# List products in the bank of the transposed values, the first softmax begun in step 23 and its sums spread over the last routing

## Chip, cores and metric

One core of a Trainium2 chip runs the whole kernel. The metric is device time in microseconds for one launch; the kernel before took 370.91 us in the median of three runs (368.12 to 375.25).

## What is computed

Three stages on 3,072 tokens (batch 4 x 768) of width 384 (8 heads x 48):

```python
# 1. linear attention with a decaying state, per (batch, head)
y[:, :, t] = r_t @ (state + u*k_t v_t^T);   state = w*state + k_t v_t^T
# 2. MoE, one of 8 experts per token, only where x @ w_skip > 0
probs  = softmax(xc @ w_gate);  e = argmax;   x = xc + probs[e] * relu(xc @ w1[e]) @ w2[e]
# 3. soft MoE with 32 slots: d is a softmax over the tokens (axis 0)
logits = x @ phi;  d = softmax(logits, axis=0);  slots = d.T @ x
out    = softmax(logits, axis=1) @ experts(slots)
```

## The kernel before

The order of the instructions on every engine is written out by hand (a manual schedule): each engine runs its instructions in the order in which the program emits them, and semaphores hold it where data or a buffer is not ready.

**The first loop** (`for i in range(NT)`, 24 steps) does the attention. Step i takes 128 positions of one batch row. On TensorE it emits `scores(i)` (L630, tile sc; then L635), `trx(i-2)` (L722, turns finished values; ScalarE copies them to x), `bonus(i)` (L652), `inter(i-1)` (L703), `upd(i)` (L649) and `av(i-1)` (L713). VectorE does `prep` (L612, L613), `past` (L676) and `amask` (L683), GpSimd the products of L615, L621, L659 and L671 and the one-hot masks `hots` (L756). Between them the routing of stage 2 goes on for groups of four steps: `route1` (L789, tile lgt), `route2` (tile lgp), `route2b`, `route3`, `places`/`gates` and `route4` (L908 to L910, emitted in steps 9, 13, 17 and 21). `gathered(g)` (L762) multiplies the tokens' numbers with their one-hot masks, for four groups of steps; the products land in PSUM as tile lip, and ScalarE casts them (L764). It is emitted right behind `bonus` in steps 13, 17 and 22 and once more behind `av` in step 22.

**PSUM banks** are shared by name. Tag "r" is one bank: lgt, lgp, lip, c4pt and others take it in turn, and a new tile waits until the last reader of the tile before it is done. In groups 0 to 3 the tile lgp also holds small scratch values (`spare`), and `route4` reads one of them (m) in L909. Tag "t" is another single bank: `trx` takes it in every step, and its only reader is ScalarE's copy (L723).

**The softmax over tokens** is built in pieces. For the first 16 steps' tokens the greatest logits are turned (L1030, c4pt, in bank "r"), reduced (L1004), spread over a diagonal (L1006, dgt), and after the loop multiplied by ones (L1105, mrt) so that every partition has them; then GpSimd subtracts (L1117), ScalarE takes Exp (L1121), and a `Weighted` object (L122, tile dpst) sums x with these weights in 16 products. The last eight steps' tokens form a second group, `gv` (c4pv, mrpv, tile dpsv).

**Last routing and start of the experts.** After the loop the last two rows are routed: `direct` (L809), `route2b(6)`, `route3(6)`, masks `hots(6)` on VectorE, `listed` (L773), the list idg (L1125); GpSimd gathers the rows of expert 0 by it (L1148, tile xg), `gtr(0)` (L1201) turns them, and `mm1` (L1213 to L1216) begins the 32 blocks of the expert phase, with `act` (hh on ScalarE, hlo on VectorE, L1224) and `mm2` (L1238 to L1240). `lows` (L956) makes the low halves of four weight blocks (early[0] to early[3]: a and b of block 0, a and b of block 1) ahead of the phase. `warm` (L492) issues products whose results nobody reads.

Of the kernel before, what the change touches and what calls it, by code (L numbers as in the profile page):

```python
# [8 lines left out]
F32 = mybir.dt.float32  # L9
# [3 lines left out]
AF = mybir.ActivationFunctionType  # L13
ALU = mybir.AluOpType
AX = mybir.AxisListType
# [4 lines left out]
P = 128  # L20
# [5 lines left out]
CAP = 256  # L26
# [439 lines left out]
def tile_main(ctx, tc, rk, kv, wu, wcat, phi, w1, w2, v1, v2, r_in, k_in, v_in, w_in, u_in, wcn, out, dbg=None, force=False):  # L466
    nc = tc.nc
# [3 lines left out]
    mk = fst.enter_context(tc.tile_pool(name="mk", bufs=1, side="right"))  # L471
# [16 lines left out]
    def warm(pool, tag, n):  # L488

        wp = pool.tile([P, 2, 4 * P], F32, tag=tag, name="wp")[:, 0] if tag == "y" else pool.tile([P, 4 * P], F32, tag=tag, name="wp")  # L490
        for _ in range(n):
            nc.tensor.matmul(wp, ones, ones.rearrange("p (o n) -> p o n", o=1).to_broadcast([P, 4, P]), start=True, stop=True)  # L492
# [168 lines left out]
    def moved(j):  # L661
        t = T[j]
        if j < NT - B:
            t["us"] = sp[j][1] if j < B else wk.tile([PR, 4, D], F32, tag="us", name=f"us{j}")
            nc.scalar.copy(t["us"], t["up"])
# [12 lines left out]
    def amask(j):  # L678
        t = T[j]
        if "at" not in t:  # L680
            past(j)
        at = t["at"]
        nc.vector.copy_predicated(  # L683
            at,
            ident_i.rearrange("s (a o t) -> s a o t", a=1, o=1).to_broadcast([P, 2, 4, P]),
            t["dtk"].rearrange("s (p o r) -> s r p o", o=1, r=32)[:, 0:2].to_broadcast([P, 2, 4, P]),
        )
# [17 lines left out]
    def av(j):  # L705
        t = T[j]
        c, b = divmod(j, B)
        yv, kvt, at = t["yv"], t["kv"], t["at"]
        for p in range(4):
            for f in range(2):  # L710
                h, g = 2 * p + f, f ^ (p < 2)
                m = 64 if c == 0 and f == 0 else D
                nc.tensor.matmul(yv[64 * f : 64 * f + m, p // 2, p % 2, :], kvt[:, 1, h * D : h * D + m], at[:, g, p, :], start=(c == 0 and p % 2 == 0), stop=(p % 2 == 1))  # L713
        if b == 0:
            yts[c] = ry.tile([PR, 4, B, P], F32, tag="yt", bufs=2, name=f"yt{c}")
        nc.scalar.copy(yts[c][:, :, b, :].rearrange("d (k q) t -> d k q t", k=2), yv)  # L716
# [21 lines left out]
    def tokens(g, eng):  # L738

        j0, nb = GR[g]  # L740
        o = tok[g % 2] if g < 4 else tok8[:, j0 - 16 : j0 - 16 + nb]
        sh = [P, nb, 2, E]
        eng.tensor_mul(
            o[:, :, 0:16].rearrange("t b (r e) -> t b r e", r=2),
            RT[g]["oh"].rearrange("t b (o e) -> t b o e", o=1).to_broadcast(sh),
            tj[:, :, j0 : j0 + nb].rearrange("t r (b o) -> t b r o", o=1).to_broadcast(sh),
        )
# [9 lines left out]

    def gathered(g):

        li = ps.tile([P, CAP], F32, tag="r", name=f"lip{g}")  # L760
        for b in range(B):
            nc.tensor.matmul(li[32 * b : 32 * b + 32, :], tok[g % 2][:, b, :], HOT[g][:, b, :], start=True, stop=True)  # L762
        LI.append(ry.tile([P, CAP], BF16, tag="li", name=f"li{g}"))
        nc.scalar.copy(LI[g], li)  # L764
# [63 lines left out]
    def route2b(g):  # L828
        c, (j0, nb) = g, GR[g]
        sh = [P, nb, E]  # L830
        r = RT[c]
        lg = r["lg"]
        if g < 6:
            nc.vector.tensor_add(lg, lg, r["lgp"][:, :, 64:106])
        else:
            lg = r["lgp"]
        gl = lg[:, :, 0:E]
        mx = spare(c, "mx", 42, 43)
        nc.vector.tensor_reduce(mx, gl, axis=AX.X, op=ALU.max)
        m = r["m"] = spare(c, "m", 43, 44) if j0 < 16 else m8[:, j0 - 16 : j0 - 16 + nb]  # L840
        nc.vector.tensor_scalar(m, lg[:, :, 8:9], 0.0, None, op0=ALU.is_gt)
        dd = rt.tile(sh, F32, tag="dd", name=f"dd{c}")
        nc.vector.tensor_sub(dd, gl, mx.to_broadcast(sh))
        wm = spare(c, "wm", 44, 52)
        nc.vector.tensor_mul(wm, w8.rearrange("t (o e) -> t o e", o=1).to_broadcast(sh), m.to_broadcast(sh))
        ex = r["ex"] = rt.tile(sh, F32, tag="ex", name=f"ex{c}")
        nc.scalar.activation(ex, dd, AF.Exp)
        t8 = spare(c, "t8", 52, 60)
        nc.vector.scalar_tensor_tensor(t8, dd, 0.0, wm, op0=ALU.is_equal, op1=ALU.mult)
        m2 = rt.tile([P, nb, 1], F32, tag="m2", name=f"m2{c}")  # L850
        nc.vector.tensor_reduce(m2, t8, axis=AX.X, op=ALU.max)
        oh = r["oh"] = rtile(g, "oh", oh8, BF16)
        nc.vector.scalar_tensor_tensor(oh, t8, 0.5, m2.to_broadcast(sh), op0=ALU.max, op1=ALU.is_equal)
# [20 lines left out]
    def gates(g):  # L874
        j0, nb = GR[g]
        se = spare(g, "se", 61, 62)
        nc.vector.tensor_reduce(se, RT[g]["ex"], axis=AX.X, op=ALU.add)
        yield
        nc.vector.tensor_scalar(se, se, 1.0e-9, None, op0=ALU.add)
        yield  # L880
        nc.vector.reciprocal(gt[:, j0 : j0 + nb], se)
        yield

    def places(g):
        j0, nb = GR[g]
        r = RT[g]
        r2 = rt.tile([P, nb, E], F32, tag="r2", name=f"r2{g}")
        nc.vector.tensor_mul(r2, r["rp"], r["oh"])
        yield
        sl = r["sl"] = rt.tile([P, nb, 1], F32, tag="sl", name=f"sl{g}")  # L890
        nc.vector.tensor_reduce(sl, r2, axis=AX.X, op=ALU.add)
        yield

    def weave(order, **steps):
        for c in order:
            next(steps[c])
# [57 lines left out]
    def lows(nm, n, sl):  # L954
        hv, lv = WS[nm, n]
        nc.vector.tensor_sub(lv, sl, hv.bitcast(F32))  # L956
# [18 lines left out]
    if True:  # L975
        for i in range(NT):
# [10 lines left out]
            if i > 1:  # L987
                trx(i - 2)
            bonus(i)
            if i in (13, 17, 22):  # L990
                gathered(len(LI))
            if i == 21:
                route1(4)
            if rok and rb == 3 or i == 22:
# [6 lines left out]
                route2(4)  # L1001
            if i == 23:
                past(23)
                nc.vector.tensor_reduce(mcs[:, 0:1], c4pt, axis=AX.X, op=ALU.max)  # L1004
                dgt = rt.tile([32, 32], F32, tag="dg", bufs=1, name="dgt")
                nc.vector.tensor_scalar(dgt, ident[0:32, 0:32], mcs[0:32, 0:1], None, op0=ALU.mult)  # L1006
                route2(5)
            if rok and rb == 1 and rc < 4:
                route1(rc)
# [15 lines left out]
            if i > 0:  # L1025
                av(i - 1)
            if i == 22:
                gathered(3)
                c4pt = ps.tile([P, P], F32, tag="r", name="c4pt")
                nc.tensor.transpose(c4pt, c4t.rearrange("p q s -> p (q s)"), ident)  # L1030
            moved(i)
            amask(i)
            if i == 22:
                weave("pgpgg", g=gates(4), p=places(4))
                tokens(4, nc.gpsimd)
                hots(4, range(4), nc.gpsimd)
            decayed(i)
# [48 lines left out]
        stored(20, 2)  # L1086
        inter(23)
        route2b(5)
        av(23)
        route3(5, prev=(4,), place=T[23]["rp"][:, 0 : 2 * E])  # L1090
        weave("ppggg", g=gates(5), p=places(5))
# [9 lines left out]
        trx(23, "tp", pc)  # L1101
        stored(23, 1)
        direct(6, 1)
        mrt = pc.tile([P, 1, 32], F32, tag="tp", name="mrpt")
        nc.tensor.matmul(mrt.rearrange("p o s -> p (o s)"), onesf[0:32], dgt, start=True, stop=True)  # L1105
        nc.scalar.copy(lx[:, 0:1, :], mrt)
        idp = ps.tile([P, 2, E], F32, tag="r", name="idp")
        for g in range(4):
            for k in range(2):
# [3 lines left out]
        route2b(6)  # L1113
        tokens(6, nc.gpsimd)
        route3(6, "ud", (4, 5))
        warm(pc, "tp", 2)
        nc.gpsimd.tensor_sub(ltm[:, 0:16, :], ltm[:, 0:16, :], lx[:, 0:1, :].to_broadcast([P, 16, 32]))  # L1117
        weave("gggpp", g=gates(6), p=places(6))
        nc.sync.dma_start(out=g_d.rearrange("(p j) n -> p j n", j=NT), in_=gt)
        hots(6, range(2), nc.vector)  # L1120
        nc.scalar.activation(ltm[:, 0:16, :], ltm[:, 0:16, :], AF.Exp)  # L1121
        w1g = Weighted(nc, "t", pc, "ds", mk, ltm, 16, lambda j: x[:, j])
        listed(22)
        listed(23)
        nc.vector.tensor_copy(idg, idp)  # L1125
# [35 lines left out]
        gates_of(1)  # L1161
        gv = Group("v", cmax2, ltm[:, 16:24, :], 8, lambda j: x[:, 16 + j], lx[:, 1:2, :], mcs[:, 1:2])
        gv.first()
        w1g.some(8)
        gv.second()
        lows(*early[0])
        w1g.some(4)
        gv.rows()
        nc.vector.tensor_copy(gv.mrow, gv.mrp)
        nc.vector.tensor_sub(gv.lg, gv.lg, gv.mrow.to_broadcast([P, gv.nt, 32]))  # L1170
        nc.scalar.activation(gv.lg, gv.lg, AF.Exp)
        DS = {"t": w1g.done()}
        for i in (1, 2, 3):
            lows(*early[i])

        cntp = pc.tile([P, E + 1], F32, tag="tp", name="cntp")
# [123 lines left out]
        V[k] = vload(nc, hl, tag, 2, k, v1, v2)  # L1300

    if True:
        warm(pc, "y0", 3)
        DS["v"] = gv.sums().done()
        warm(pc, "y0", 3)
        nc.gpsimd.memset(x2[:, :, DM : DM + 1], 1.0)
        gtr(0, (0, 1, 2), ("tp", "tp", "hp"))
        mxc = mk.tile([P, 1], F32, name="mxc")
        nc.vector.tensor_reduce(mxc, cnt[:, 0:E].rearrange("p e o -> p (e o)"), axis=AX.X, op=ALU.max)
        okc = mk.tile([P, 1], F32, name="okc")  # L1310
# [301 lines left out]
```

## Time and profile before

| What | Value |
|---|---|
| median of 3 runs | 370.91 us (368.12 to 375.25) |
| profiled execution | 368.68 us, span 366.9 us |
| mean granted clock of TensorE | 0.965 of full speed |
| TensorE busy | 341.8 us (93% of the span) |
| VectorE / ScalarE / GpSimd busy | 248.4 / 149.4 / 151.5 us |
| DMA | 85.18 MB, mean 232 GB/s |

The span runs from the first to the last instruction of the profiled execution. "Busy" sums the time in which an engine executes; a bracket behind a row of a timeline tells how long the engine had been idle before it and what released it. The clock is given as the share of full speed that was granted.

### The profile page before, as it was taken

How to read it: one execution, taken by the hardware profiler on the slowest of the kernel's cores; microseconds unless marked ns; L12 is line 12 of the kernel's file. 1: busy time of each engine (PE TensorE's matmuls, PEld its weight loads, DVE VectorE, ACT ScalarE, POOL GpSimd, SP SyncE). 2: the span in 40 equal slices, each digit the busy share in tenths (PEclk: the TensorE clock that was granted, in tenths of full speed). 3: DMA queues.
4: the chain of work that ended last, by engine and by line, in shares of the span. 5: the costliest groups of instructions: out<-in, count | busy, mean ns of one | idle time of the engine just before them, and what ended most of it. 6: DMA issues, size and time to landing. Idle time of an engine off the chain costs nothing. (4 is left out here: it accounts for less than half of the span.)

```text
span 366.9 us, 8790 instructions
## 1 busy us (share of the span) xinstructions
PE 341.8 (93%) x3522; PEld 273.0 (74%) x3522; DVE 248.4 (68%) x496; ACT 149.4 (41%) x322; POOL 151.5 (41%) x191
## 2 busy tenths in 40 slices
PE   8899999979799978999999999999999999999870
PEld 3577686767578657399999999999899999734360
DVE  5988898947957975776665756757476765416660
ACT  1133334313324323445555546454455552321270
POOL 3857669777664643750424233242324202020000
PEclk9999999969989999899999999999999999999985
DMA  8985657554645972569879687887875548669486
GB/s 218 265 237 188 191 180 240 178 184 145 226 141 172 372 283 92 171 224 343 284 242 306 208 301 254 277 282 256 294 249 163 178 161 276 244 212 372 153 300 224
DMA packets 45744, 85.18 MB, mean 232 GB/s; under 512 B 3854, under 2 KB 26688, under 8 KB 45696
## 3 DMA queue, kind: packets, MB, share of 16 engines
q1 hardware_dynamic: 43040, 80.63, 66.7%
q0 software_dynamic: 2128, 3.74, 3.8%
q8 instruction: 30, 0.49, 0.5%
q10 hardware_dynamic: 528, 0.16, 0.2%
q14 instruction: 18, 0.15, 0.1%
HBM read 74.49 MB, written 10.10 MB: 231 GB/s over the span
## 5 line engine op out<-in xcount | busy, mean ns | idle before, releaser
L1213 PE MATMUL hp<-xhl,wa 128*128 128x256 f32 x192 | 48.5, 289 | 0.2 <-ACT xhl L1203 0.2
L1214 PE MATMUL hp<-xhl,wa 128*128 128x256 f32 x192 | 47.1, 282 | 0.0
L956 DVE TENSOR_TENSOR wa<-w,wa 128x768 fp32r<-128x768 f32 x32 | 30.6, 955 | 22.0 <-ACT wa L968 22.0
L1238 PE MATMUL yp<-wb,hh 128*128 128x384 f32 x128 | 45.1, 352 | 0.0
L1240 PE MATMUL yp<-wb,hlo 128*128 128x384 f32 x128 | 42.9, 335 | 0.0
L1239 PE MATMUL yp<-wb,hh 128*128 128x384 f32 x128 | 42.9, 335 | 0.0
L1148 POOL DMA_INDIRECT xg<-x_d,idg x16 | 19.8, 1238 | 53.4 <-DVE x L1246 41.9
L676 DVE TENSOR_TENSOR at<-sc,mask 128x1024 f32<-128x1024 f32 x24 | 29.3, 1220 | 15.1 <-PE sc L630 15.1
L1268 POOL DMA_INDIRECT lt_d<-lsr,ids x16 | 17.7, 1107 | 52.5 <-ACT xhl L1203 29.9
L1213 PEld LDWEIGHTS hp<-xhl,wa 128*128 128x128 f32 x192 | 36.5, 190 | 0.5 <-ACT xhl L1203 0.5
L1214 PEld LDWEIGHTS hp<-xhl,wa 128*128 128x128 f32 x192 | 36.5, 190 | 0.0
L683 DVE COPY_PREDICATED at<-ident,ud 128x1024 f32<-128x1024 int32 x24 | 31.5, 1311 | 4.1 <-PE ud L652 1.8
L615 POOL TENSOR_TENSOR pd<-rkb 112x512 f32<-112x512 f32 x24 | 30.7, 1280 | 7.7 <-DMA rkb<-in_rk_dram 5.3
L956 DVE TENSOR_TENSOR wb<-w,wb 128x768 fp32r<-128x768 f32 x32 | 30.9, 965 | 3.0 <-ACT wb L968 2.6
L968 ACT CAST wb<-w 128x768 fp32r<-128x768 f32 x32 | 26.8, 837 | 8.8 <-PE yp L1240 5.0
L716 ACT COPY yt<-yp 112x512 f32<-112x512 f32 x24 | 14.0, 585 | 40.0 <-PE yp L713 40.0
L1224 DVE SCALAR_TENSOR_TENSOR hlo<-hp,hh 128x512 fp32r<-128x512 f32 x32 | 22.0, 687 | 12.0 <-ACT hh L1223 11.3
L1223 ACT ACTIVATE hh<-hp 128x512 fp32r<-128x512 f32 x32 | 19.1, 598 | 26.2 <-PE hp L1216 26.0
L630 PE MATMUL sc<-rks 48*128 48x128 f32 x384 | 29.6, 296 | 0.0
L713 PE MATMUL yp<-at,kvt 128*48 128x128 f32 (+1 forms) x384 | 28.7, 286 | 0.0
L630 PEld LDWEIGHTS sc<-rks 48*128 48x128 f32 x384 | 24.9, 198 | 4.8 <-issue 3.3
L1216 PE MATMUL hp<-xhl,wa 128*128 128x256 f32 x192 | 28.2, 283 | 0.0
(335 smaller groups left out, 719.8 us busy)
## 6 DMA issues: line engine op xcount, KB each, us to landing
w<-in_w_dram SPq DMA_DIRECT2D x32, 768.0 KB
v<-in_v_dram SPq DMA_DIRECT2D x29, 768.0 KB
rkb<-in_rk_dram SPq DMA_DIRECT2D x24, 448.0 KB
kvt<-in_kv_dram SPq DMA_DIRECT2D x24, 384.0 KB
x_d<-x SPq DMA_DIRECT2D x5, 768.0 KB
out_dram<-ob SPq DMA_DIRECT2D x5, 768.0 KB
x<-in_v_dram SPq DMA_DIRECT2D x2, 768.0 KB
ltt<-in_v_dram SPq DMA_DIRECT2D x1, 768.0 KB
```

Source lines behind the costliest of these rows:

```text
L615: nc.gpsimd.tensor_mul(t["pd"], rkt[:, 0], rkt[:, 1])
L630: nc.tensor.matmul(sc[:, hf, p, :], ks[r0 : r0 + D, p, :], rs[r0 : r0 + D, p, :], start=True, stop=True)
L676: nc.vector.tensor_mul(at, t["sc"], mask.rearrange("s (a o t) -> s a o t", a=1, o=1).to_broadcast([P, 2, 4, P]))
L683: nc.vector.copy_predicated(at, ident_i.rearrange("s (a o t) -> s a o t", a=1, o=1).to_broadcast([P, 2, 4, P]), t["dtk"].rearrange("s (p o ...
L713: nc.tensor.matmul(yv[64 * f : 64 * f + m, p // 2, p % 2, :], kvt[:, 1, h * D : h * D + m], at[:, g, p, :], start=(c == 0 and p % 2 == 0), ...
L956: nc.vector.tensor_sub(lv, sl, hv.bitcast(F32))
L1213: nc.tensor.matmul(hp[:, f, :], hi[:, k, fs], xh[:, k, :], start=(k == 0 and f == 0), stop=False)
L1214: nc.tensor.matmul(hp[:, f, :], lo[:, k, fs], xh[:, k, :], start=False, stop=False)
L1216: nc.tensor.matmul(hp[:, f, :], hi[:, k, fs], xl[:, k, :], start=False, stop=(k == 2 and f == 1))
L1238: nc.tensor.matmul(YP[e][bl], hh[:, f, bs], hi[:, f, :], start=st, stop=False)
L1239: nc.tensor.matmul(YP[e][bl], hh[:, f, bs], lo[:, f, :], start=False, stop=False)
L1240: nc.tensor.matmul(YP[e][bl], hlo[:, f, bs], hi[:, f, :], start=False, stop=en)
```

## The change

`gathered` moves from behind `bonus` to behind `moved` (the end of TensorE's part of a step), its tile goes from bank "r" to bank "t", and its steps become 13, 17, 21 and 22. The reduction of c4pt and dgt move from step 23 to step 22. The product with ones (mrt), its copy and GpSimd's subtraction move from behind the loop into step 23, in bank "t"; Exp moves behind `route2b(5)`. Six of the 16 products of dpst move into the last routing, where two `warm` products stood; the other ten are issued five and five. Six more `warm` products are taken out. Of the four `lows`, blocks a are made after the second group's Exp, blocks b behind `gtr(0)`.

```diff
--- before.py
+++ after.py
@@ -757,7 +757,7 @@
 
     def gathered(g):
 
-        li = ps.tile([P, CAP], F32, tag="r", name=f"lip{g}")
+        li = ps.tile([P, CAP], F32, tag="t", name=f"lip{g}")
         for b in range(B):
             nc.tensor.matmul(li[32 * b : 32 * b + 32, :], tok[g % 2][:, b, :], HOT[g][:, b, :], start=True, stop=True)
         LI.append(ry.tile([P, CAP], BF16, tag="li", name=f"li{g}"))
@@ -987,8 +987,6 @@
             if i > 1:
                 trx(i - 2)
             bonus(i)
-            if i in (13, 17, 22):
-                gathered(len(LI))
             if i == 21:
                 route1(4)
             if rok and rb == 3 or i == 22:
@@ -1001,9 +999,10 @@
                 route2(4)
             if i == 23:
                 past(23)
-                nc.vector.tensor_reduce(mcs[:, 0:1], c4pt, axis=AX.X, op=ALU.max)
-                dgt = rt.tile([32, 32], F32, tag="dg", bufs=1, name="dgt")
-                nc.vector.tensor_scalar(dgt, ident[0:32, 0:32], mcs[0:32, 0:1], None, op0=ALU.mult)
+                mrt = ps.tile([P, 1, 32], F32, tag="t", name="mrpt")
+                nc.tensor.matmul(mrt.rearrange("p o s -> p (o s)"), onesf[0:32], dgt, start=True, stop=True)
+                nc.scalar.copy(lx[:, 0:1, :], mrt)
+                nc.gpsimd.tensor_sub(ltm[:, 0:16, :], ltm[:, 0:16, :], lx[:, 0:1, :].to_broadcast([P, 16, 32]))
                 route2(5)
             if rok and rb == 1 and rc < 4:
                 route1(rc)
@@ -1025,13 +1024,17 @@
             if i > 0:
                 av(i - 1)
             if i == 22:
-                gathered(3)
                 c4pt = ps.tile([P, P], F32, tag="r", name="c4pt")
                 nc.tensor.transpose(c4pt, c4t.rearrange("p q s -> p (q s)"), ident)
             moved(i)
+            if i in (13, 17, 21, 22):
+                gathered(len(LI))
             amask(i)
             if i == 22:
                 weave("pgpgg", g=gates(4), p=places(4))
+                nc.vector.tensor_reduce(mcs[:, 0:1], c4pt, axis=AX.X, op=ALU.max)
+                dgt = rt.tile([32, 32], F32, tag="dg", bufs=1, name="dgt")
+                nc.vector.tensor_scalar(dgt, ident[0:32, 0:32], mcs[0:32, 0:1], None, op0=ALU.mult)
                 tokens(4, nc.gpsimd)
                 hots(4, range(4), nc.gpsimd)
             decayed(i)
@@ -1086,6 +1089,7 @@
         stored(20, 2)
         inter(23)
         route2b(5)
+        nc.scalar.activation(ltm[:, 0:16, :], ltm[:, 0:16, :], AF.Exp)
         av(23)
         route3(5, prev=(4,), place=T[23]["rp"][:, 0 : 2 * E])
         weave("ppggg", g=gates(5), p=places(5))
@@ -1101,9 +1105,6 @@
         trx(23, "tp", pc)
         stored(23, 1)
         direct(6, 1)
-        mrt = pc.tile([P, 1, 32], F32, tag="tp", name="mrpt")
-        nc.tensor.matmul(mrt.rearrange("p o s -> p (o s)"), onesf[0:32], dgt, start=True, stop=True)
-        nc.scalar.copy(lx[:, 0:1, :], mrt)
         idp = ps.tile([P, 2, E], F32, tag="r", name="idp")
         for g in range(4):
             for k in range(2):
@@ -1113,13 +1114,11 @@
         route2b(6)
         tokens(6, nc.gpsimd)
         route3(6, "ud", (4, 5))
-        warm(pc, "tp", 2)
-        nc.gpsimd.tensor_sub(ltm[:, 0:16, :], ltm[:, 0:16, :], lx[:, 0:1, :].to_broadcast([P, 16, 32]))
+        w1g = Weighted(nc, "t", pc, "ds", mk, ltm, 16, lambda j: x[:, j])
+        w1g.some(6)
         weave("gggpp", g=gates(6), p=places(6))
         nc.sync.dma_start(out=g_d.rearrange("(p j) n -> p j n", j=NT), in_=gt)
         hots(6, range(2), nc.vector)
-        nc.scalar.activation(ltm[:, 0:16, :], ltm[:, 0:16, :], AF.Exp)
-        w1g = Weighted(nc, "t", pc, "ds", mk, ltm, 16, lambda j: x[:, j])
         listed(22)
         listed(23)
         nc.vector.tensor_copy(idg, idp)
@@ -1161,16 +1160,15 @@
         gates_of(1)
         gv = Group("v", cmax2, ltm[:, 16:24, :], 8, lambda j: x[:, 16 + j], lx[:, 1:2, :], mcs[:, 1:2])
         gv.first()
-        w1g.some(8)
+        w1g.some(5)
         gv.second()
-        lows(*early[0])
-        w1g.some(4)
+        w1g.some(5)
         gv.rows()
+        DS = {"t": w1g.done()}
         nc.vector.tensor_copy(gv.mrow, gv.mrp)
         nc.vector.tensor_sub(gv.lg, gv.lg, gv.mrow.to_broadcast([P, gv.nt, 32]))
         nc.scalar.activation(gv.lg, gv.lg, AF.Exp)
-        DS = {"t": w1g.done()}
-        for i in (1, 2, 3):
+        for i in (0, 2):
             lows(*early[i])
 
         cntp = pc.tile([P, E + 1], F32, tag="tp", name="cntp")
@@ -1300,11 +1298,11 @@
         V[k] = vload(nc, hl, tag, 2, k, v1, v2)
 
     if True:
-        warm(pc, "y0", 3)
         DS["v"] = gv.sums().done()
-        warm(pc, "y0", 3)
         nc.gpsimd.memset(x2[:, :, DM : DM + 1], 1.0)
         gtr(0, (0, 1, 2), ("tp", "tp", "hp"))
+        for i in (1, 3):
+            lows(*early[i])
         mxc = mk.tile([P, 1], F32, name="mxc")
         nc.vector.tensor_reduce(mxc, cnt[:, 0:E].rearrange("p e o -> p (e o)"), axis=AX.X, op=ALU.max)
         okc = mk.tile([P, 1], F32, name="okc")
```

## Rows read from the trace of the kernel before

**Rows 1.** TensorE's waits: who waited for whom, total us, times, longest

```profile
PE lip L762 <- DVE ltt L909: 5.6, 2, 2.8
```

**Rows 2.** Timeline, TensorE, step 13: start us, us, line, tiles [idle before]

```profile
75.70 0.40 PE L762 MATMUL lip<-hot,tok 128*32 128x256 bf16 x4 [2.81 <-DVE ltt L909]
```

**Rows 3.** Timeline of VectorE, step 13

```profile
75.37 0.28 DVE L909 SCALAR_TENSOR_TENSOR ltt<-lgp,lg 128x128 f32<-128x128 f32 x1
```

**Rows 4.** Windows: stretch, length, busy us (PE, PEld, DVE, ACT, POOL), clock, DMA

```profile
51.04:61.45 10.41, 10.35 (x163) 7.34 (x162) 10.03 (x23) 3.68 (x9) 9.72 (x13) 1.00 0.82 241
70.60:86.76 16.16, 13.35 (x167) 9.72 (x166) 10.24 (x20) 4.06 (x10) 11.43 (x14) 0.79 0.49 155
95.91:110.92 15.01, 12.19 (x168) 8.94 (x167) 10.25 (x20) 4.06 (x10) 10.69 (x13) 0.89 0.52 169
75.10:81.90 6.80, 6.20 (x72) 5.06 (x75) 2.21 (x5) 1.18 (x3) 4.71 (x7) 0.50 0.37 112
102.40:105.80 3.40, 3.40 (x34) 3.04 (x30) 0.86 (x2) 0.81 (x2) 2.27 (x4) 0.50 0.12 20
146.80:150.10 3.30, 3.30 (x21) 0.82 (x17) 1.50 (x5) 2.83 (x4) 2.05 (x2) 0.50 0.77 257
...
160.40:293.00 132.60, 132.60 (x972) 127.56 (x971) 87.05 (x143) 72.64 (x136) 42.55 (x38) 1.00 0.77 255
```

**Rows 5.** Timeline of TensorE, steps 22 and 23

```profile
131.70 0.33 PE L1030 MATMUL c4pt<-ident,c4t 128*128 128x128 f32 x1 [0.74 <-ACT li L764]
...
134.65 1.08 PE L789 MATMUL lgt<-yt,wcs 112*64 112x256 f32 x8 [1.52 <-DVE mcs L1004]
```

**Rows 6.** Timeline of VectorE, steps 21 to 23

```profile
125.85 1.33 DVE L87 COPY c4t<-cmax 128x128 f32<-128x128 f32 x1
...
132.84 0.18 DVE L881 RECIPROCAL gt<-se 128x4 f32<-128x4 f32 x1
...
134.31 0.28 DVE L1004 TENSOR_REDUCE mcs<-c4pt 128x1 f32<-128x128 f32 x1
```

**Rows 7.** Timeline of GpSimd, step 22 and the last routing

```profile
132.82 3.61 POOL L756 TENSOR_SCALAR hot<-ipl,sl 128x256 bf16<-128x256 f32 x4 [3.81 <-DVE se L879]
...
144.66 1.26 POOL L1117 TENSOR_TENSOR ltt<-ltt,lx 128x512 f32<-128x512 f32 x1
```

**Rows 8.** Timeline of TensorE, last routing to the experts

```profile
143.18 0.40 PE L1105 MATMUL mrpt<-dgt,onesf 32*128 32x32 f32 x2
...
144.56 0.17 PE L872 MATMUL rp<-oh,tri 128*128 128x16 bf16 x1
...
146.13 0.52 PE L773 MATMUL idp<-tok,hot 128*128 128x8 bf16 x8 [0.95 <-DVE hot L756]
146.64 2.74 PE L122 MATMUL dpst<-x,ltt 128*32 128x385 f32 x16
149.31 0.48 PE L936 MATMUL c4pv<-ident,c4v 128*128 128x128 f32 x1
...
152.82 1.50 PE L122 MATMUL dpsv<-x,ltt 128*32 128x385 f32 x16
...
154.91 0.82 PE L1201 MATMUL xtp<-ident,xg 128*128 128x128 f32 x6
...
160.73 0.34 PE L1240 MATMUL yp<-wb,hlo 128*128 128x384 f32 x1
```

**Rows 9.** Timeline of VectorE, the same stretch

```profile
147.92 0.23 DVE L931 COPY c4v<-cmax 128x128 f32<-128x128 f32 x1
...
151.17 0.17 DVE L1169 COPY lx<-mrpv 128x32 f32<-128x32 f32 x1
...
159.12 0.69 DVE L1224 SCALAR_TENSOR_TENSOR hlo<-hp,hh 128x512 fp32r<-128x512 f32 x1 [0.70 <-issue]
```

**Rows 10.** Timeline of ScalarE, the same stretch

```profile
151.84 0.42 ACT L1171 ACTIVATE ltt<-ltt 128x256 f32<-128x256 f32 x1 [2.21 <-DVE ltt L1170]
```

**Rows 11.** DMA queues from 149.5 to 152.3 us: packets, MB, share of 16 engines

```profile
q0 software_dynamic: 128, 0.39, 48.8%
```

## Prediction

> **What bounds the kernel now.** I read the page first: TensorE is busy in nearly every slice, so a microsecond is won only where TensorE stands still or runs at the lower of its two clock levels. The list of its waits says where it stands still. The largest entry by far is two waits of 2.8 us, both of the list product lip for VectorE's L909 [rows 1]. The timelines show one of the two: lip begins at 75.70 us after 2.81 us of idleness [rows 2], and L909 had ended at 75.37 + 0.28 = 75.65 us [rows 3]. L909 computes nothing that lip reads. It reads m, which lies in the tile lgp, in bank "r", and lip wants that bank. So this is a wait for a bank, and behind lip stands everything else that TensorE has to do in that step.
>
> Then the windows, cut at the first score product of steps 9, 11, 13, 15, 17 and 19. Steps 9 and 10 do the same work as 13 and 14 and as 17 and 18, only without lip. They take 10.41 us at full clock, against 16.16 and 15.01 us [rows 4]. The difference is more than the idleness, because behind each wait the granted clock was 0.50, which is 1.2 instead of 2.4 GHz: for 6.8 us behind the first and for 3.4 us behind the second [rows 4]. The reader should also see what is near its limit in the fast pair: VectorE is busy 10.03 of 10.41 us and GpSimd 9.72 [rows 4]. Nothing can go faster than that pair.
>
> From step 21 to step 23 the timelines of TensorE and VectorE show two more waits, 0.74 us ahead of c4pt and 1.52 us ahead of lgt [rows 5], both for bank "r" again. At the end of the routing TensorE waits 0.95 us for masks, and from 146.64 to the turning of the gathered rows at 154.91 us it works in order without a gap, 3.3 us of it at the low clock [rows 4, 8]. After that, from 160.4 to 293 us, it is busy throughout at full clock [rows 4], so what comes earlier there moves everything behind it.
>
> **The change part by part.**
>
> Lip in bank "t", behind moved. The bank's tile before it is trx's, whose only reader, ScalarE's copy, runs long before `av` ends; L909 has no part in it. Steps 13 and 14 should then cost what 9 and 10 cost plus lip itself. Lip's row spans 0.40 us at the low clock [rows 2]; I take 0.22 for its share. The gain is 16.16 - 10.41 - 0.22 = 5.53 us, and for 17 and 18 it is 15.01 - 10.41 - 0.22 = 4.38 us: together **9.9 us**. Bounds: at least the idleness alone less lip, 5.6 - 0.4 = 5.2 us, if the clock stays low all the same; at most 10.35 us, if lip costs nothing. VectorE's work in the two pairs is 10.24 and 10.25 us [rows 4], 0.2 us over the fast pair's, which leaves it room within 10.63 us. What is queued behind lip now: the cast on ScalarE comes behind the copies of yt and us, and `trx` of the next step waits for it in bank "t". Between lip and that `trx` TensorE has a whole `scores` to do, so I cost this wait at nothing; without that cover it costs at most one cast a time, in four steps.
>
> Step 22 and 23. Without lip in bank "r" c4pt needs no cast, and its 0.74 us go. They are absorbed, since the next scores only feed VectorE, which is still busy with the masks of step 22. What counts is lgt. It now waits until L1004 has read c4pt, which ends at 134.31 + 0.28 = 134.59 us because L1004 stands behind `past(23)`. Moved ahead of it, behind the reciprocal that ends at 132.84 + 0.18 = 133.02 us [rows 6], it ends at about 133.3, and lgt starts at about 133.4 instead of 134.65 us [rows 5]: 1.25 us earlier. Against that, mrt goes into TensorE's row in the same step, at 0.40 us [rows 8]; where it stood the routing chain of VectorE was the bound, so nothing comes back there. Net **0.85 us**, between 0 and 1.25. GpSimd's subtraction (1.26 us) comes behind the four masks, which run until 132.82 + 3.61 = 136.43 us [rows 7], and so ends near 137.7 us, ahead of the next masks. Exp on ScalarE finds it done. Their cover is GpSimd's and ScalarE's idleness in step 23; without it Exp would hold back the last copy of yt.
>
> One risk in this place shows in a row: the copy c4t took 1.33 us [rows 6], its twin c4v 0.23 us [rows 9]. Dgt, moved to 133.3 us, now runs beside the four masks. If it is held as long as c4t, 1.1 us, `past(23)` slips by that, but `amask(23)` behind it waits for `bonus(23)`, some 2 us after lgt, so the sum loses at most 0.3 us. The Trainium skill ("SBUF — State Buffer", section "SBUF: two separate sides") says that VectorE and GpSimd share one port pair as an exclusive lock, held for a whole instruction, which fits the two copies and speaks against moving dgt beside the masks. By that rule dgt waits for one mask to end, at most 3.61/4 = 0.9 us, and the sum by the rule is the same as by the row, within the 0.3 us.
>
> Six products in the last routing. Route3's last product ends at 144.56 + 0.17 us, the last lists start at 146.13 us: room for 1.40 us. The products run as 12 passes, at 1.50/16 us each at full clock and 2.74/16 at low [rows 8], so 1.13 or 2.06 us: hidden, or 0.65 us late.
>
> From the list to the experts. TensorE's row of work ahead of gtr(0) loses six products and six `warm`. What is late next is the second group's chain. C4v ends at 147.92 + 0.23 = 148.15 us [rows 9]; c4pv followed at 149.31 us only because eight products ran first [rows 8]. It can start 1.16 us earlier, and with one `lows` less in VectorE's row the chain to Exp, which ends at 151.84 + 0.42 us [rows 10], moves as much, to 151.1 us. Dpsv then takes 1.50 us, and gtr(0) starts at 152.6 instead of 154.91 us: 2.3 us earlier. The gathered rows are no bound: their 0.39 MB have landed by 152.3 us [rows 11]. At the low clock dpsv takes 2.74 us and five products in front 1.7 us, and nearly all of it is gone. A low stretch like that at 146.8 us is likely here again, and partly under waits. I take **1.4 us**, between 0 and 2.3.
>
> Blocks b behind gtr(0). Two `lows` of about 0.95 us now stand ahead of hlo. VectorE was idle 0.70 us before hlo, and `mm2` used it at 160.73 us, 0.92 us after its end [rows 8, 9]; 1.9 us against 1.6 leaves a wait of **0.2 us**, between 0 and 1.2.
>
> Sum: 9.9 + 0.85 + 1.4 - 0.2 = 12.0 us (11.95). The span goes from 366.9 to 354.9 us, the profiled execution from 368.68 to 356.7. That execution lies 2.2 us below the median of 370.91, and the median less 12.0 is 358.9. I predict **357.5 us**, between the two.
>
> **The rivals.**
>
> *Steps gain only their idleness.* The bank is free, but the clock stays low for as long as now, or VectorE and GpSimd, busy over 93% in the fast pair [rows 4], set the pace in four steps in a row. Gain 5.2 to 8 us with the rest at half: 361 to 365 us. Against it: steps 9 and 10 ran exactly so at full clock.
>
> *No change.* Lip waits as long in its new place, for a reader of bank "t" or for masks, and the wait has only moved. Then 0.85 + 1.2 us are left at most: 367 to 371 us. Against it: the 0.05 us between L909's end and lip's start [rows 2, 3], twice, names the bank.
>
> *Slower: the low clock stays in the expert phase.* Eight `warm` products are gone, and TensorE now waits for Exp shortly before it. From 160.4 us it works 132.6 us at full clock [rows 4]. Each 2 us of low clock there cost 1 us, so the gain is gone from 24 us on, and 39 us make it 2% slower, about 378 us. Against it: the three low stretches shown ended after 6.8, 3.4 and 3.3 us with TensorE busy [rows 4]. The Trainium skill ("TensorE: Matmul & The Clock Gate", section "Part 1: The HAM clock gate (the "warmup" mystery)") calls the throttled state the default that activity releases, which speaks against taking `warm` out, though the products that come instead are activity too. By that rule alone the stretch from the list to the experts would win 0 instead of 1.4 us, and the sum would be 10.6 us.
>
> **How the numbers follow.** The forecast has 0.72, with a range of its own of 354 to 360.5 us; a still larger gain 0.02; steps with their idleness alone 0.14; no change 0.09; slower 0.03. The sum with every bound at its best is 10.35 + 1.25 + 2.3 = 13.9 us; from the lowest run, 368.12, that gives 354.2. So the low end is 353.5 us. The high end is 363.5 us, which takes in most of the first rival and leaves out 0.17 above and 0.02 below. Two per cent, which is about what a measurement can tell, is 7.4 us: the forecast and most of the first rival are faster by more, 0.85; within 2% 0.12; slower 0.03.
>
> **What would show it.** Right: no wait of lip for L909; the pairs 13 and 14, 17 and 18 take 10.4 to 10.9 us at clock 1.00; lgt starts right behind the reduction of c4pt, and about 1 us earlier than now counted from the scores of step 21; gtr(0) 2 to 4 us earlier counted from the same point; hlo of block 0 is followed by a wait of TensorE under half a microsecond. Wrong: lip with a wait of another name; a clock of 0.50 in steps 13 to 19; a granted clock under 1.00 after mm1's start; a VectorE without gaps in steps 13 to 19 with pairs over 11 us.

## The result and the profile after

The changed kernel takes 356.24 us in the median (354.62 to 356.74), the kernel before 369.51 in the same rounds (366.78 to 375.25): a ratio of 0.966, with an interval of 0.958 to 0.974. In a second group of runs it was 354.83 against 370.12 us, 0.959 (0.954 to 0.964). The profiled execution took 356.74 us with a span of 354.9 us, 12.0 us less than before.

TensorE's waits in the changed kernel, in the columns of [rows 1]:

```profile
...
PE yp L1238 <- DVE hlo L1222: 1.2, 1, 1.2
PE lgt L789 <- DVE mcs L1035: 1.2, 1, 1.2
...
PE dpsv L122 <- ACT ltt L1170: 0.9, 1, 0.9
PE ud L652 <- ACT dts L637: 0.8, 2, 0.4
PE xtp L1199 <- DMA xg<-x_d,idg: 0.7, 1, 0.7
```

The entry of [rows 1] is gone: lip waits for nobody. In its place stand three entries that the kernel before did not have, hlo, dpsv and xtp, each a part of the last stretch.

The windows of the changed kernel, cut at the first scores of steps 13, 15, 17 and 19 (the first two lines), then at the scores of step 21, lgt of step 23, the list idg, the first expert product and the first product of block 2, in the columns of [rows 4]:

```profile
70.17:80.69 10.52, 10.52 (x168) 7.42 (x167) 10.07 (x20) 3.96 (x10) 9.84 (x13) 1.00 0.80 238
89.83:100.35 10.52, 10.52 (x168) 7.42 (x167) 10.09 (x20) 3.96 (x10) 9.83 (x13) 1.00 0.76 240
109.04:122.80 13.76, 12.48 (x168) 8.36 (x166) 13.20 (x35) 4.87 (x12) 7.16 (x9) 1.00 1.04 379
122.80:134.85 12.05, 11.86 (x187) 8.88 (x191) 7.25 (x31) 6.95 (x17) 6.67 (x9) 1.00 0.35 127
134.85:143.12 8.27, 6.31 (x56) 2.43 (x55) 5.07 (x14) 2.48 (x6) 6.03 (x6) 1.00 0.67 184
143.12:151.08 7.96, 6.79 (x49) 6.47 (x50) 7.79 (x20) 3.13 (x6) 5.46 (x8) 1.00 0.72 256
```

The two pairs of steps take 10.52 us each at full clock, against 16.16 and 15.01 [rows 4]: 5.64 + 4.49 = 10.13 us. In this execution the granted clock is 1.00 in every one of these stretches; none of the three low stretches of [rows 4] is left. From the scores of step 21 to the first product of block 2 it takes 13.76 + 12.05 + 8.27 + 7.96 = 42.0 us, and before it took 162.47 - 119.61 = 42.9 us by the same marks. So the second half of the change brought only 0.8 us in this execution. The remaining 1 us of the 12.0 came ahead of step 9 (0.4) and behind block 2 (0.6), where nothing was changed.

TensorE and VectorE of the changed kernel, from lgt of step 23 to the last stretch, first the one and then the other, as in [rows 8] and [rows 9]:

```profile
122.80 1.08 PE L789 MATMUL lgt<-yt,wcs 112*64 112x256 f32 x8 [1.16 <-DVE mcs L1035]
...
133.04 1.49 PE L122 MATMUL dpst<-x,ltt 128*32 128x385 f32 x12
134.46 0.35 PE L773 MATMUL idp<-tok,hot 128*128 128x8 bf16 x8
134.74 1.48 PE L122 MATMUL dpst<-x,ltt 128*32 128x385 f32 x10
...
136.62 1.48 PE L122 MATMUL dpst<-x,ltt 128*32 128x385 f32 x10
138.03 0.40 PE L944 MATMUL mrpv<-dgv,onesf 32*128 32x32 f32 x2
...
139.63 1.50 PE L122 MATMUL dpsv<-x,ltt 128*32 128x385 f32 x16 [0.85 <-ACT ltt L1170]
141.06 0.55 PE L1199 MATMUL xtp<-ident,xg 128*128 128x128 f32 x3
142.33 0.55 PE L1199 MATMUL xtp<-ident,xg 128*128 128x128 f32 x3 [0.72 <-DMA xg<-x_d,idg]
...
149.21 0.44 PE L1238 MATMUL yp<-wb,hlo 128*128 128x384 f32 x1 [1.17 <-DVE hlo L1222]
```

```profile
133.86 0.62 DVE L756 TENSOR_SCALAR hot<-ipl,sl 128x256 bf16<-128x256 f32 x2
...
137.05 0.23 DVE L940 TENSOR_SCALAR dgv<-ident,mcs 32x32 f32<-32x32 f32 x1
...
146.54 1.54 DVE L1317 TENSOR_SCALAR emp<-cnt,pio 128x8 f32<-128x8 f32 x2
...
148.48 0.68 DVE L1222 SCALAR_TENSOR_TENSOR hlo<-hp,hh 128x512 fp32r<-128x512 f32 x1
```

The reader sees the list go straight behind the six products, dpsv wait for Exp, the second half of the turning of the gathered rows wait for them, and TensorE stand before hlo, which is late because the two small operations of L1317 took 1.54 us.

### The profile page after: what moved, and what is told of

Read it like the earlier page. It is cut to its first block, busy times and chain, and to the rows that moved or that the text cites. A ratio compares the mean times of both kernels' runs of the same rounds, so it can differ in the third digit from the quotient of the medians.

```text
span 354.9 us, 8778 instructions
## 1 busy us (share of the span) xinstructions
PE 333.5 (94%) x3514; PEld 267.1 (75%) x3514; DVE 248.6 (70%) x496; ACT 149.1 (42%) x322; POOL 150.8 (42%) x191
## 5 line engine op out<-in xcount | busy, mean ns | idle before, releaser
L1237 PE MATMUL yp<-wb,hh 128*128 128x384 f32 x128 | 42.9, 335 | 0.0
L630 PE MATMUL sc<-rks 48*128 48x128 f32 x384 | 27.9, 285 | 0.0
L756 POOL TENSOR_SCALAR hot<-ipl,sl 128x256 bf16<-128x256 f32 x22 | 20.2, 924 | 16.1 <-DVE gt L881 7.8
L713 PE MATMUL yp<-at,kvt 128*48 128x128 f32 (+1 forms) x384 | 26.9, 275 | 0.0
```

The source lines that it names most:

```text
L630: nc.tensor.matmul(sc[:, hf, p, :], ks[r0 : r0 + D, p, :], rs[r0 : r0 + D, p, :], start=True, stop=True)
L1237: nc.tensor.matmul(YP[e][bl], hh[:, f, bs], lo[:, f, :], start=False, stop=False)
```

## The experiments

Each profile is of one execution; the ratios come from three rounds beside the kernel before.

**The list products alone.** The kernel before with only this:

```diff
-        li = ps.tile([P, CAP], F32, tag="r", name=f"lip{g}")
+        li = ps.tile([P, CAP], F32, tag="t", name=f"lip{g}")
...
-            if i in (13, 17, 22):
-                gathered(len(LI))
...
-                gathered(3)
...
             moved(i)
+            if i in (13, 17, 21, 22):
+                gathered(len(LI))
```

> The kernel before with the list products alone changed (bank "t", behind moved, steps 13, 17, 21, 22); softmax, lows and warm as before. Theory (the wait for bank "r" and the low clock behind it are the main part): 10.1 us less than before, as steps 13 to 18 lose 5.64 + 4.49 us in the changed kernel, and the granted clock is 1.00 in steps 13 to 19. Rival (the softmax's move carries the gain): under 4 us less.

Measured: ratio 0.971 (0.963 to 0.979), 359.9 us in the median against 370.87. Windows of its profile, the first a pair of steps:

```profile
70.36:80.88 10.52, 10.52 (x167) 7.42 (x167) 10.09 (x20) 3.96 (x10) 9.83 (x13) 1.00 0.74 238
125.70:129.10 3.40, 3.40 (x33) 2.42 (x33) 1.88 (x6) 0.95 (x3) 0.38 (x1) 0.51 0.33 123
136.00:146.20 10.20, 9.25 (x61) 2.79 (x64) 7.25 (x15) 4.58 (x8) 7.27 (x7) 0.50 0.53 158
```

The steps gain what the theory says, to 0.01 us. The profiled span is 359.0 us, though, 7.9 and not 10.1 us less: two stretches of low clock, 3.4 and 10.2 us long, now lie in the routing and behind it, where the kernel before had one of 3.4. The four executions lay between 357.45 us, at a mean clock of 0.985, and 360.84, at 0.970.

**The bank alone, the place alone.** First bank "t" with the places as before, then bank "r" with lip behind `moved` in steps 13 and 17 (22 as before):

```diff
-        li = ps.tile([P, CAP], F32, tag="r", name=f"lip{g}")
+        li = ps.tile([P, CAP], F32, tag="t", name=f"lip{g}")
```

> The kernel before with lip in bank "t" and its places as before (behind bonus). Theory (the bank is the cause): lip waits only for ScalarE's copy of trx, about 0.4 us in each of steps 13 and 17, so 9 to 10 us less than before. Rival (the place in the step is the cause): lip waits 2 us or more, and less than 3 us are gained.

```diff
-            if i in (13, 17, 22):
+            if i == 22:
                 gathered(len(LI))
...
             moved(i)
+            if i in (13, 17):
+                gathered(len(LI))
```

> The kernel before with lip left in bank "r" and moved behind moved in steps 13 and 17 alone. Theory (the place alone would nearly do, as L909 ends at 75.65 us and TensorE would come to lip at about 75.1): a wait of about 0.5 us in each of the two steps, 8.5 to 9.5 us less than before. Rival (only the bank counts): the wait stays near 2.8 us and nothing is gained.

The wait of lip with the bank alone, and its window of steps 13 and 14:

```profile
PE lip L762 <- ACT x L723: 0.7, 2, 0.3
```

```profile
70.01:80.93 10.92, 10.59 (x168) 7.51 (x167) 10.09 (x20) 4.07 (x10) 10.23 (x13) 1.00 0.75 230
```

The same two with the place alone:

```profile
PE lip L762 <- DVE ltt L909: 1.5, 2, 0.8
```

```profile
69.83:81.17 11.34, 10.59 (x168) 7.50 (x167) 10.07 (x20) 4.05 (x10) 10.66 (x14) 1.00 0.71 221
```

Measured: 0.971 (0.963 to 0.979) and 0.969 (0.960 to 0.978). Either half brings nearly all of it: the pair falls from 16.16 us [rows 4] to 10.92 with the bank alone and to 11.34 with the place alone, and to 10.52 with both. With the place alone lip still waits for L909, but TensorE comes to it later, 0.75 us before L909 ends, and behind its two waits of 0.75 and 0.77 us the clock stayed at 1.00. Both rivals fall.

**The wait filled.** Ten products that nobody reads, ahead of lip:

```diff
+            if i in (13, 17):
+                warm(ps, "y", 10)
             if i in (13, 17, 22):
                 gathered(len(LI))
```

> The kernel before with ten products that nobody reads (128 x 512, some 2.2 us) ahead of lip in steps 13 and 17, inside its wait. Theory (two costs, idleness and the low clock behind it): lip starts as late as before, the clock stays at 1.00, and 16.16 - 10.41 - 0.22 - 2.81 = 2.7 us and 15.01 - 10.41 - 0.22 - 2.82 = 1.6 us are gained, 4.3 us in all. Rival (the slow steps behind are not from the clock but from VectorE and GpSimd catching up): no gain.

TensorE in step 13, and behind it the windows of the two pairs of steps:

```profile
72.82 2.32 PE L492 MATMUL wp<-ones 128*128 128x512 bf16 x10
75.82 0.29 PE L762 MATMUL lip<-hot,tok 128*32 128x256 bf16 x4 [0.67 <-DVE ltt L909]
```

```profile
70.70:84.11 13.41, 12.74 (x177) 8.40 (x176) 10.25 (x20) 4.05 (x10) 11.41 (x14) 1.00 0.58 187
93.26:106.68 13.42, 12.74 (x178) 8.41 (x177) 10.26 (x20) 4.05 (x10) 10.72 (x13) 1.00 0.59 190
```

The wait for L909 is still there, only filled, and the pairs fall by 2.75 + 1.59 = 4.34 us; 4.3 were expected. So the 10.13 us are about 5.8 us of standing still and 4.3 us of low clock behind it. The ratio is 0.987 (0.978 to 0.997), and 4.34 of 370.87 us would make 0.988. The profiled execution as a whole does not show the gain: its span is 366.8 us, with 17.1 us of low clock between step 21 and the experts.

**The rest alone.** The changed kernel with the list products as before:

```diff
-        li = ps.tile([P, CAP], F32, tag="t", name=f"lip{g}")
+        li = ps.tile([P, CAP], F32, tag="r", name=f"lip{g}")
...
-            if i in (13, 17, 21, 22):
-                gathered(len(LI))
```

(and `gathered` behind `bonus` in steps 13, 17 and 22 and ahead of c4pt, as before)

> The changed kernel with the list products as before (bank "r", behind bonus, steps 13, 17, 22 and 22). Theory (the rest brings 12.0 - 10.1 = 1.9 us, less the cast that c4pt waits for again): 1 to 2.5 us less than the kernel before, 9.5 to 11 more than the changed one, and two waits of 2.8 us as before. Rival (the softmax's move carries the gain): 6 us or more less than before.

Measured: 0.990 (0.980 to 0.9999), a gain that is hardly clear of the noise; a span of 365.0 us, 1.9 less than before, with the two waits of lip at 5.6 us in all, as in [rows 1]. With 0.971 for the list products the product is 0.961, which agrees with the 0.959 and 0.966 of the whole change.

**The same kernel again.**

> The changed kernel once more, beside the runs of this group. All theories: 356.2 us as in its first runs, within 1 us.

354.83 us, span 353.4 us. Most stretches repeat to 0.02 us, but not the last one. L1317 and hlo in this execution:

```profile
146.10 0.34 DVE L1317 TENSOR_SCALAR emp<-cnt,pio 128x8 f32<-128x8 f32 x2
...
146.84 0.68 DVE L1222 SCALAR_TENSOR_TENSOR hlo<-hp,hh 128x512 fp32r<-128x512 f32 x1
```

From the first expert product to block 2 it takes 6.74 us here, 7.96 in the first execution and 6.50 before. So the wait of 1.17 us for hlo belongs to the first execution. What stays in both is 0.24 us. The wait for the gathered rows is not there either:

```profile
141.10 0.90 PE L1199 MATMUL xtp<-ident,xg 128*128 128x128 f32 x6
142.68 0.39 PE L1211 MATMUL hp<-xhl,wa 128*128 128x256 f32 x1 [0.69 <-ACT xhl L1201]
```

All six turning products run in a row, and the first expert product waits for ScalarE's cast instead. It comes 7.79 us after the list, against 8.27 us in the first execution and 9.29 before. From the scores of step 21 to block 2 it takes 40.3 us here, 2.5 us less than before, where the first execution gave 0.8.

**The small operations later; GpSimd's zeroing later.** Two edits of the changed kernel for the wait before hlo. The first emits the block mxc to nv behind the activations of block 1, the second puts GpSimd's work on spx and nvt into block 5:

```diff
-        mxc = mk.tile([P, 1], F32, name="mxc")
...
             if n == 1:
+                mxc = mk.tile([P, 1], F32, name="mxc")
```

> The changed kernel with the block of small operations on the counts (mxc to nv) moved from ahead of hlo of block 0 to behind the activations of block 1. In the changed kernel TensorE waits 1.17 us for hlo. Theory (the small operations, held 1.2 us in L1317, make hlo late): the wait goes and the kernel takes 1.2 to 1.4 us less than the changed one. Rival (the two lows in front make it late): at most 0.3 us less.

```diff
-                spx = spread(nc, cn, mk2)
+                spx = mk2.tile([P, 2, 3, 4, 32], F32, name="spx")
...
+            if n == 5:
+                nc.gpsimd.memset(spx, 0.0)
...
```

> The changed kernel with GpSimd's zeroing of spx and its work on nvt moved to block 5, so that GpSimd does not write while VectorE does the small operations. Theory (L1317 took 1.54 us instead of 0.34 because it was held until GpSimd's zeroing ended): L1317 is back near 0.34 us, the wait for hlo falls from 1.17 to 0.2 us, and the kernel takes about 1.0 us less. Rival (the two lows in front make hlo late): L1317 and the wait stay.

Measured: 354.2 us (0.959) and 355.04 us (0.960), not to be told from the changed kernel's 354.83 in the same group. In the first the wait is gone, and 6.50 us to block 2 are back. In the second L1317 took 0.34 us and the stretch 6.70 us, but so it did in the unchanged kernel's second execution. The first edit shows that the small operations, behind the two `lows`, cost 0.24 us ahead of hlo, now and then 1.4; the second tells nothing by itself. What held L1317 shows when the profiles are laid side by side. GpSimd's zeroing of spx in the first execution:

```profile
147.28 0.76 POOL L149 MEMSET spx<- 128x768 f32 x1
```

L1317 ended at 148.08 us, 0.04 us after the zeroing (147.28 + 0.76 = 148.04 us). Of the thirteen profiles, five have the two operations at the same time, and in each of them the line of L1317 ends 0.03 to 0.05 us after the zeroing: 1.54 us here and in the run with the six products late (below), 1.33 with the wait filled, 0.56 with the place alone, 0.48 with the list products alone. In the other eight it takes 0.34 us. By these coincidences VectorE was held until the zeroing ended; no run forced one. In three of the five L1317 had begun 0.5 to 0.7 us ahead of the zeroing, beside GpSimd's last gather; why it was held from there on is not shown.

**c4pt in bank "t".** The first of these two kernels with the banks of c4pt and the last list product exchanged:

```diff
-        li = ps.tile([P, CAP], F32, tag="t", name=f"lip{g}")
+        li = ps.tile([P, CAP], F32, tag="r" if g == 3 else "t", name=f"lip{g}")
...
-                c4pt = ps.tile([P, P], F32, tag="r", name="c4pt")
+                c4pt = ps.tile([P, P], F32, tag="t", name="c4pt")
```

> The kernel of the run before this one with c4pt in bank "t" and the last list product in bank "r", so that lgt of step 23 waits for a cast instead of the reduction of c4pt. Theory (the 1.16 us wait of lgt sits on the path): 0.8 to 1.1 us less than the run before this one, 2.0 to 2.5 less than the changed kernel. Rival (VectorE's row sets the end of step 23 anyway): no difference.

354.37 us, 0.958 (0.953 to 0.963): no difference. TensorE in its profile, and behind it a window:

```profile
119.86 1.16 PE L630 MATMUL sc<-rks 48*128 48x128 f32 x16
120.95 1.08 PE L789 MATMUL lgt<-yt,wcs 112*64 112x256 f32 x8
...
131.33 2.71 PE L122 MATMUL dpst<-x,ltt 128*32 128x385 f32 x12
133.98 0.36 PE L773 MATMUL idp<-tok,hot 128*128 128x8 bf16 x8
```

```profile
130.40:133.80 3.40, 3.24 (x39) 1.25 (x35) 1.99 (x12) 3.32 (x6) 0.24 (x1) 0.50 0.31 77
```

The wait of lgt is gone, and lgt starts 1.2 us earlier, as expected. But in this execution the clock is low from 130.4 us on, the six products take 2.71 instead of 1.49 us, and the list behind them comes 1.2 us late. The gain was given back in the next stretch. It shows neither theory wrong: the wait was on the path, and its worth was lost to the clock. The one execution at a mean clock of 0.988 took 353.29 us; that of the run before at the same clock took 353.99.

**Warm products back; the six products out of the routing.**

```diff
+        warm(pc, "y0", 3)
         DS["v"] = gv.sums().done()
+        warm(pc, "y0", 3)
```

> The changed kernel with the two groups of three warm products put back around dpsv. Theory (the clock stayed at 1.00 without them, and they fit in TensorE's waits of 0.85 us for Exp and 0.72 us for the gathered rows): within 0.3 us of the changed kernel, clock 1.00. Rival (they keep the clock up and the one execution profiled was lucky): the changed kernel is slower than this one by 1 us or more in its median.

```diff
-        w1g.some(6)
+        warm(pc, "tp", 2)
...
-        w1g.some(5)
+        w1g.some(8)
         gv.second()
-        w1g.some(5)
+        w1g.some(8)
```

> The changed kernel with two warm products in the last routing instead of the six products of the first group; the 16 products come eight and eight behind the list, as TensorE has room there. Theory (behind the list the second group's chain and the gathered rows are the bound): within 0.3 us of the changed kernel if the clock stays at 1.00. Rival (the products in the routing are what keeps the clock up at its end): a stretch at 0.50 behind the list as in the kernel before, and 0.5 to 1.7 us more.

With `warm` back: 355.81 us, 0.964 (0.956 to 0.973), the changed kernel's own range. Its profile has a low stretch of 3.4 us from 133.0 us on, ahead of the products put back, in a part where the two kernels are the same. So that stretch comes and goes between executions, and the six `warm` are worth nothing that can be measured. With the six products late: 357.79 us, 0.971 (0.963 to 0.980), four executions from 357.42 to 358.29, all above every one of the changed kernel's eight. Its last stretch on TensorE, and behind it a window of it:

```profile
132.82 0.59 PE L492 MATMUL wp<-ones 128*128 128x512 bf16 x2
134.13 0.52 PE L773 MATMUL idp<-tok,hot 128*128 128x8 bf16 x8 [0.71 <-DVE hot L756]
134.58 2.11 PE L122 MATMUL dpst<-x,ltt 128*32 128x385 f32 x16
```

```profile
135.30:138.70 3.40, 3.40 (x25) 0.86 (x21) 1.28 (x4) 0.07 (x1) 2.28 (x2) 0.50 0.84 279
```

The wait before the list is back, behind it the clock falls as in [rows 4, 8], and most of the 16 products run at that clock, eight ahead of c4pv and eight ahead of mrpv, the two links of the second group's chain. From the list to the turning it takes 7.63 us here and 6.21 in the changed kernel. Not all of the difference in time comes from there: in this profile L1317 took 1.54 us again, and TensorE waited 1.15 us for hlo.

## Why the prediction was right, and where its terms were off

The forecast was 12.0 us off the profiled execution, and 12.0 came. It was right for the reason that it gave, in its largest term. That the figure came to the tenth is luck: 1.0 of the 12.0 us came from stretches where nothing was changed, and the small terms, 0.85 + 1.4 - 0.2 = 2.05 us in the forecast, brought 0.8 us in the first execution and 2.5 in the second.

- **Lip: 9.9 us, measured 10.13.** The mechanism is shown by the bank alone and the place alone, its two halves by the filled wait. The fast pair of steps was the right measure: 10.52 us with lip in it against 10.41 without. I had costed lip at 0.22 us; the pair grew by 0.11. The cast in bank "t" cost nothing, as said.
- **Lgt: 1.25 us, measured 1.28** (13.76 us from the scores of step 21, before 15.04). Mrt cost 0.33 us where 0.40 was taken. Dgt took 0.23 us, though the masks beside it had been running for 0.4 us; it was not held. The rule of the Trainium skill that spoke against its place ("SBUF — State Buffer", section "SBUF: two separate sides") is not borne out by this row. The Trainium skill names there only some of VectorE's operations, those in a two-port mode or with two inputs from SBUF, which the prediction left out; no row tells whether dgt is one. Another row of the same execution agrees with it (last section).
- **The masks of the last routing** gained 0.33 us that I had not seen: VectorE's two masks took 0.62 instead of 0.95 us once GpSimd's subtraction no longer ran beside them. So it is in all thirteen profiles: 0.95 or 0.96 us in the five with the subtraction there, 0.61 or 0.62 in the eight without. This gave back what mrt had cost: the masks end 11.68 us after the start of lgt in both kernels. The sum missed what a moved GpSimd operation frees.
- **The six products: hidden, or 0.65 us late.** They took 1.49 us, not 1.13, and were just hidden; at the low clock 2.71 us, which makes the list 1.2 us late. The price per pass was the wrong measure: in the changed kernel 10, 12 and 16 passes take 1.48, 1.49 and 1.50 us, and in the kernel before 8 passes took 0.86:

```profile
151.03 0.86 PE L122 MATMUL dpst<-x,ltt 128*32 128x385 f32 x8
```

  `Weighted` sends product j to strip j % 4 of the output, so 5, 6 and 8 products (of two passes each) are two rounds of up to four, and 4 are one. The times fit a price per round; no run varied the number alone. The step gave the six products no worth of their own, and that was wrong: with them late the kernel takes 1.5 to 3 us more, and its profile has a low clock behind the wait that they had filled. L1317 has a part in that profile too, so the 1.4 us from the list to the turning are the safer figure.
- **From the list to the experts: 1.4 us, measured 2.0 to gtr(0)** and, to the first expert product, 1.0 in the first execution and 1.5 in the second. The step that failed in the first is "the gathered rows are no bound". They had landed by 152.3 us before, and gtr(0) was predicted at 152.6: a margin of 0.3 us, and it went. GpSimd starts the gathers about 1 us after the list in both kernels, so the rows did not come earlier by more than the list did. In the second execution TensorE did not wait for them. The sum had also missed a wait in the chain to Exp: mrpv came 0.75 us after dgv was done, since five products stood before it and took 1.48 us where the price per pass gives 0.94. So Exp ended 0.85 us earlier counted from the list, not 1.16. The term's size came out near what I took, for these reasons and not for the low clock that I had put in their place.
- **Hlo: 0.2 us, measured 0.24 in one execution and 1.46 in the other** (6.74 and 7.96 us against 6.50). (The forecast's own rows give 1.90 - 1.62 = 0.28.) The upper bound of 1.2 us was nearly right for the wrong cause: not the two `lows`, but L1317 at 1.54 us, held by a GpSimd operation that no term of the sum looked at.
- **The rivals.** A clock that stays low in the steps, and a VectorE or GpSimd that sets the pace, are excluded by the two windows at 1.00. The clock in the expert phase never fell, without the `warm` products too (1.00 from 151.1 to 341 us); putting them back changed nothing. The Trainium skill's rule ("TensorE: Matmul & The Clock Gate", section "Part 1: The HAM clock gate (the "warmup" mystery)") that activity releases the lower state fits the filled wait: the clock stayed at 1.00 behind it.
- **The signs.** Lip waits for nobody, the pairs take 10.52 us at clock 1.00, and lgt and gtr(0) start 1.28 and 3.28 us earlier counted from the scores of step 21. The last sign, a wait for hlo under half a microsecond, failed in the first execution and came in the second.
- **The median** fell by 13.3 and 15.3 us in two groups, more than the 12.0 of the profiles. The kernel before varies from execution to execution with its mean clock: 366.22 us at 0.970 and 371.01 at 0.957 in one group. The profiled execution lay at the fast end of that, which the prediction had half allowed for with its 357.5.

The small edits that take out the waits before hlo and lgt do not give a kernel that can be told from the changed one.

## What to carry to other kernels

A tile that waits for a buffer of its own name waits for the last reader of the tile before it, even one emitted later; look for the reader in the trace, and move the tile to a bank whose reader is early, or to a place behind the wait. Price a wait of TensorE not by its length but by comparing the stretch with one like it that has no wait, for the lower clock behind the wait can cost nearly as much as the wait (here 4.3 us against 5.8). And a gain measured in one stretch has to be followed to the end, since a low stretch of clock can turn up in the next one.

## What the runs showed of the hardware beside this

- The low stretches of the clock do not belong to a place. From step 21 to the experts the kernel before has 3.4 us of them. With lip's waits in steps 13 and 17 gone, shortened or filled it has, in profiles, 13.6 us (the list products alone), 6.8 (the bank alone), 17.1 (the place alone), 17.1 (the wait filled) and none (the changed kernel, twice).
- The spread between executions follows the clock: between the two of the kernel before named above, 4.8 us of time go with a difference of 0.013 in the mean clock.
- VectorE can be held until an operation of GpSimd's ends, and is not always. In step 23 of the changed kernel, VectorE first and then GpSimd:

```profile
126.97 0.57 DVE L841 TENSOR_SCALAR m<-lg 128x2 f32<-128x2 f32 x1
```

```profile
126.25 1.27 POOL L1005 TENSOR_TENSOR ltt<-ltt,lx 128x512 f32<-128x512 f32 x1 [0.34 <-ACT lx L1004]
```

  Two elements a partition took 0.57 us and ended at 127.54 us, when the subtraction ended (127.52); the same line took 0.16 us in step 21. It took 0.57 us in all seven profiles where the two overlap, and 0.18 with c4pt in bank "t", where it ran ahead of the subtraction. Against that stands dgt in the same step, at 0.23 us in the middle of a mask of GpSimd's, in all eight profiles with it there:

```profile
122.69 0.23 DVE L1037 TENSOR_SCALAR dgt<-ident,mcs 32x32 f32<-32x32 f32 x1
```

```profile
122.29 3.61 POOL L756 TENSOR_SCALAR hot<-ipl,sl 128x256 bf16<-128x256 f32 x4 [3.82 <-DVE se L879]
```

- An operation of VectorE on 8 elements a partition took 0.34 us for two in one execution and 1.54 us in another of the same kernel, with GpSimd at work beside it in both: a gather in the first case, a gather and then the zeroing in the second.
